# Output projection over pairs of token tiles by Strassen's scheme, with operands in slots of finished heads

## The chip, the cores and the metric

One core of one Trainium2 chip. The metric is device time of the whole program in microseconds (us), the median of repeated runs. The engines are named as in the profile: PE (matmuls; PEld is its weight loads), DVE, ACT and POOL (elementwise work), and SP, which here only issues DMAs. A queue's own entries carry a q (SPq).

## The reference

Two independent parts, written side by side into a 2048 x 1152 output, all fp32:

```python
# A: 32 heads of 18 features, in 4 segments of 512 tokens
q, k, v = x @ wq, x @ wk, x @ wv
for s in range(4):
    p = softmax(qs @ ks.T * scale + mask)          # mask of one segment
    o = g * (phi(qs) @ M / (phi(qs) @ z)) + (1 - g) * (p @ vs)
    M, z = M + phi(ks).T @ vs, z + phi(ks).sum(0)
a = concat(o) @ wo                                 # 2048 x 576 by 576 x 576
# B: real part of a two-dimensional Fourier transform by matrices
y = Cr @ (x @ Dr.T) - Ci @ (x @ Di.T)              # Cr, Ci: 2048 x 2048
out = concat([a, y], axis=-1)
```

The line that the change concerns is `concat(o) @ wo`.

## The kernel before

All precise products are split: an fp32 operand is cut into a high part that PE takes as it is and a low part (the rest), and a product is the sum of low x high, high x low and high x high. The 576 features are four chunks of 128 and a last one of 64; that last one is stored twice over 128 partitions (`_tail_twice`), so that high and low half share one operand and two matmuls do.

A first phase (to about 240 us) projects q, k, v and looks up the memory. A second phase runs two streams in one program order. `dense()` is part B as a generator: for `ri` 0 and 1, 16 steps of `hidden`, then 16 of `sequence`, whose left operand comes in chunks (`c_load`, `c_cut`: a load to `craw`, four buffers, then `chi` by ACT and `clo` by POOL). `attention()` goes over `NP` = 64 pairs of heads, one period of eight yields each, with stages that lag: `s_fill` in the pair's own period, `f_fill` and `t_fill` 2 and 3 periods later, the products with V (`pv`) 4 later. A loop advances `attention`, and then `dense` as long as its share of estimated time is behind. `later(n, ...)` puts a call n ticks on. What `dense` has left after the last period runs alone. Every engine takes its instructions in program order; all DMAs but a few are issued by SP in program order, the transposing DMAs of `f_turn` (L789) among them.

`wo` is loaded and split in the second half of `sequence` for `ri` = 1 (`wo_load`, L715, `wo_split`, which uses `split_wk`, L124 to L130), into ten slots of the pool `wide` (32 slots of 128 x 576) that the Fourier weights have left. The attention result lies in DRAM (`od`, `odt`), transposed. The output stage is the last loop: for each of 16 token tiles of 128, `o_split` makes `oth`, `otl`, `ott` of a tile loaded two tiles ahead (`o_load`, L695 and L697: one DMA for 512 features, two for the last 64), and for each half of the 576 output columns `chain` (L84) sums 14 matmuls of 128 x 128 by 128 x 288 in one bank `d`. ACT copies the bank to `y` (L1025), and four DMAs store a tile's rows (L1031):

```python
for k in range(4):
    terms += [(hi[:, k], wl[k][:, cs]), (hi[:, k], wh[k][:, cs]), (lo[:, k], wh[k][:, cs])]
chain(o, terms + [(tl, wt1[:, cs]), (tl, wt2[:, cs])])
act.activation(y[:, cs], o, AF.Copy)
```

`open_output` gives back the attention's pool `sa` before that and opens a new one, `sb3`, for the stage. The query and key stacks of head groups (`qs0` to `qs3`, `ks0` to `ks3`) are single buffers in `sr` and `sa`.

Of the kernel before, what the change touches and what calls it, by code (L numbers as in the profile page):

```python
# [12 lines left out]
F32 = mybir.dt.float32  # L13
F32R = mybir.dt.float32r
# [3 lines left out]
OP = mybir.AluOpType  # L18
# [22 lines left out]
def infini_attention_and_fnet(ctx: ExitStack, tc: tile.TileContext, xT, wqk, w8, wv, wo, beta, xtT, cT, hT, out):  # L41
# [16 lines left out]
    def split(hi, lo, raw, lo_engine=None):  # L58
        act.activation(hi, raw, AF.Copy)
        (lo_engine or dve).tensor_tensor(lo, raw, hi.bitcast(F32), OP.subtract)  # L60
# [80 lines left out]
    def weight(mk):  # L141
        return [[mk() for _ in range(4)] for _ in range(2)] + [mk() for _ in range(2)]
# [543 lines left out]
    O, O3, OT, WO, WORAW = {}, [], {}, [], []  # L686

    def o_load(t):  # L690
        if t >= NT:
            return
        s, a = divmod(t, 4)
        o = O3[0].tile([P, 5, P], F32, name="o", bufs=3) if O3 else sb.tile([P, 5, P], F32, name="raw", tag="raw", bufs=3)
        dma(o[:, :4], od[s][:, a * P:a * P + P].rearrange("c p x -> p c x"))  # L695
        for i in range(2):
            dma(o[64 * i:64 * i + 64, 4], odt[s][64 * a:64 * a + 64])  # L697
        O[t] = o

    def o_split(t):  # L700
        if t >= NT:
            return
        o_load(t + 2)
        o = O.pop(t)
        hi = O3[0].tile([P, 4, P], F32R, name="oth", bufs=2)
        lo = O3[0].tile([P, 4, P], F32R, name="otl", bufs=2)
        tl = O3[0].tile([P, P], F32R, name="ott", bufs=2)
        split(hi, lo, o[:, :4])
        act.activation(tl, o[:, 4], AF.Copy)
        dve.tensor_tensor(tl[64:], o[64:, 4], tl[64:].bitcast(F32), OP.subtract)  # L710
        OT[t] = hi, lo, tl

    def wo_load(k):
        raw = sb.tile([P, D], F32, name="raw", tag="raw", bufs=3)
        dma(raw, wo[k])  # L715
        WORAW.append(raw)

    def wo_split(k):
        if k == 0:
            WO.extend(weight(wide_tile(D)))  # L720
        split_wk(WO, k, WORAW.pop(0), 2)

    def open_output():
        p2a.close()
        O3.append(ctx.enter_context(tc.tile_pool(name="sb3", bufs=1, reuse_waits="tile")))

    p2a = ExitStack()
    sa = p2a.enter_context(tc.tile_pool(name="sb2a", bufs=1, reuse_waits="tile"))
    PT, PV = {}, {}


# [189 lines left out]
    def attention():  # L921
        for p in range(NP + V_LAG):
# [6 lines left out]
                    fn(2 * (p - lag) + 1, *a)  # L929

            if p < 2:
                stacks(sa, p + 2)
# [58 lines left out]
    while due:  # L991
        tick()
    td = ta = 0.0
    for w in attention():
# [18 lines left out]
    for t in range(NT):  # L1013
        o_split(t + 1)
        hi, lo, tl = OT.pop(t)
        y = O3[0].tile([P, D], F32, name="y3", bufs=2)
        for h in range(2):
            cs = slice(h * 288, h * 288 + 288)
            o = ps.tile([P, 288], F32, name="d", bufs=3)
            terms = []  # L1020
            wh, wl, wt1, wt2 = WO
            for k in range(4):
                terms += [(hi[:, k], wl[k][:, cs]), (hi[:, k], wh[k][:, cs]), (lo[:, k], wh[k][:, cs])]
            chain(o, terms + [(tl, wt1[:, cs]), (tl, wt2[:, cs])])
            act.activation(y[:, cs], o, AF.Copy)  # L1025
            if h or t == NT - 1:
                cs = cs if t == NT - 1 else slice(0, D)
                for q in range(4):
                    r = 512 * (t // 4) + P * q + 32 * (t % 4)
                    queue = nc.scalar if h and t == NT - 1 and q >= 2 else nc.sync  # L1030
                    queue.dma_start(out[r:r + 32, cs], y[32 * q:32 * q + 32, cs])  # L1031


_INS = ("xT", "wqk", "w8", "wv", "wo", "beta", "xtT", "cT", "hT")
# [38 lines left out]
```

## Time and profile before

| | |
|---|---|
| median of 3 runs | 998.46 us (997.72 to 999.36) |
| span of the profiled execution | 996.2 us; no time of its own outside the span is given for it |
| median less span | 2.3 us |
| granted PE clock | 0.999 of full speed |
| PE, DVE, ACT, POOL busy | 99%, 76%, 71%, 64% of the span |
| PE's instructions | 9294 matmuls, each with a weight load |
| DMA | 208.92 MB, 80.8% of 16 engines' time |

Busy time is the union of an engine's instructions. A matmul's own duration (some 290 ns here) overlaps with its neighbours', so the price of a matmul is the distance between starts, not its duration. Rows of the chain give a start, a duration, the engine, the tile and the line. Rows of groups give count, busy time and mean duration in ns, and behind the bar the idle time before them with what ended it.

### The profile page before, as it was taken

The numbers are of one execution on the slowest core, as the hardware profiler recorded it, in microseconds if no ns is written. First come the engines' busy times: TensorE is split into PE (matmuls) and PEld (weight loads), VectorE is DVE, ScalarE is ACT, GpSimd is POOL, SyncE is SP. The second block draws the span as 40 slices with busy tenths as digits, with TensorE's granted clock in tenths as the row PEclk, the third lists the DMA queues.
The fourth block names the chain that finished last, engine by engine and source line by source line (L and its number), as shares of the span: only waits on it lengthen the run. The fifth ranks groups of instructions, "written<-read, shape, count | busy, mean of one in ns | idle before, by whom it ended". The sixth has DMA issues, their size and how long they took to land.

```text
span 996.2 us, 25590 instructions
## 1 busy us (share of the span) xinstructions
PE 986.1 (99%) x9294; PEld 924.1 (93%) x9294; DVE 753.5 (76%) x2052; ACT 712.0 (71%) x1680; POOL 636.3 (64%) x700
## 2 busy tenths in 40 slices
PE   9999999999999999999999999999999999999998
PEld 8989989899999999999999999999999999999998
DVE  6657667594678777888898888888889899998321
ACT  7757575653887877878788888877777787777243
POOL 2657676675767677666766777766766767667000
PEclk9999999999999999999999999999999999999999
DMA  7537456767588898899999988779999999989455
GB/s 252 187 117 257 172 180 242 234 232 228 150 174 217 215 251 222 207 237 215 245 238 238 222 214 199 178 200 226 230 216 229 238 235 242 240 191 200 128 148 142
DMA packets 305615, 208.92 MB, mean 210 GB/s; under 512 B 206289, under 2 KB 260433, under 8 KB 305489
## 3 DMA queue, kind: packets, MB, share of 16 engines
q1 hardware_dynamic: 305248, 207.15, 80.8%
q8 instruction: 73, 1.20, 0.5%
q14 instruction: 54, 0.43, 0.2%
q10 hardware_dynamic: 240, 0.14, 0.0%
HBM read 121.32 MB, written 57.93 MB: 180 GB/s over the span
## 4 chain that ended last, share of the span: by engine, by line
PE 84%; DVE 6%; ACT 5%; issue 2%; DMA 2%; POOL 1%; SPq 0%; POOLq 0%; DVEq 0%; ACTq 0%
PE d L583 38%; PE s L744 7%; PE d L84 6%; PE v L84 4%; PE pv L862 4%; PE qk L250 4%; PE d L628 3%; PE d L629 3%; PE d L630 3%; PE pv L863 2%; PE m L363 1%; PE t L818 1%; PE qk L84 1%; DVE r L276 1%; PE t L821 1%
## 5 line engine op out<-in xcount | busy, mean ns | idle before, releaser
L750 DVE CUSTOM_DVE_ANT_0 s<-s,causal 128x128 f32<-128x128 f32 (+3 forms) x512 | 248.1, 504 | 94.0 <-PE s L744 84.8
L456 POOL TENSOR_TENSOR clo<-craw,chi 128x512 fp32r<-128x512 f32 x158 | 217.1, 1374 | 94.4 <-ACT chi L451 66.4
L583 PE MATMUL d<-wide,chi 128*128 128x288 f32 x1408 | 261.7, 303 | 0.0
L583 PEld LDWEIGHTS d<-wide,chi 128*128 128x128 f32 x1408 | 210.7, 188 | 2.7 <-issue 1.1
L583 PE MATMUL d<-wide,clo 128*128 128x288 f32 x704 | 173.3, 313 | 0.0
L784 POOL TENSOR_TENSOR hl<-pf,hl 128x768 f16<-128x768 f32 x64 | 112.6, 1759 | 69.3 <-ACT hl L780 58.7
L830 ACT ACTIVATE phi<-t 128x384 f16<-128x384 f32 x128 | 61.8, 483 | 103.8 <-PE t L827 103.8
L744 PE MATMUL s<-ks,qs 108*128 108x128 bf16 (+3 forms) x512 | 132.8, 303 | 2.7 <-DVE negm L750 2.1
L773 ACT ACTIVATE pf<-s,nb 128x128 f32<-128x128 f32 (+3 forms) x256 | 128.3, 527 | 6.2
L583 PE MATMUL d<-ab,chi 128*128 128x288 f32 x640 | 123.3, 302 | 0.0
L845 DVE TENSOR_TENSOR plo<-pf,phi 128x384 f16<-128x384 f32 (+1 forms) x128 | 122.9, 960 | 0.0
L583 PEld LDWEIGHTS d<-wide,clo 128*128 128x128 f32 x704 | 117.8, 189 | 1.9 <-issue 0.5
L451 ACT ACTIVATE chi<-craw 128x512 fp32r<-128x512 f32 x160 | 100.2, 627 | 6.1 <-DMA craw<-xtT 3.3
L831 ACT ACTIVATE pf<-t 128x384 f32<-128x384 f32 (+1 forms) x192 | 99.5, 518 | 5.9 <-PE t L818 5.5
L583 PEld LDWEIGHTS d<-ab,chi 128*128 128x128 f32 x640 | 97.8, 189 | 0.5
L780 ACT ACTIVATE hl<-pf 128x768 f16<-128x768 f32 (+1 forms) x128 | 87.4, 729 | 2.0
L583 PE MATMUL d<-ab,clo 128*128 128x288 f32 x320 | 83.0, 308 | 0.0
L628 PE MATMUL d<-wide,chi 128*128 128x288 f32 x256 | 81.3, 318 | 0.0
L629 PE MATMUL d<-wide,chi 128*128 128x288 f32 x256 | 75.7, 296 | 0.0
L630 PE MATMUL d<-wide,clo 128*128 128x288 f32 x256 | 75.6, 295 | 0.0
L845 POOL TENSOR_TENSOR plo<-pf,phi 128x384 f16<-128x384 f32 x64 | 61.4, 959 | 13.8 <-ACT pf L831 13.3
L784 DVE TENSOR_TENSOR hl<-pf,hl 128x512 f16<-128x512 f32 x64 | 69.4, 1084 | 0.1
(214 smaller groups left out, 2500.1 us busy)
## 6 DMA issues: line engine op xcount, KB each, us to landing
craw<-cT SPq DMA_DIRECT2D x128, 256.0 KB
ks<-kd SPq DMA_DIRECT2D x32, 432.0 KB
qs<-qd SPq DMA_DIRECT2D x32, 432.0 KB
craw<-xtT SPq DMA_DIRECT2D x32, 320.0 KB
vd<-vs SPq DMA_DIRECT2D x16, 440.0 KB
vst<-vd SPq DMA_DIRECT2D x32, 220.0 KB
qd<-p SPq DMA_DIRECT2D x16, 384.0 KB
kd<-p SPq DMA_DIRECT2D x16, 384.0 KB
```

What stands on the lines that cost most here:

```text
L84: pe.matmul(o, a, b, start=n == 0, stop=n == len(terms) - 1)
L451: act.activation(hi, raw[:, :4], AF.Copy)
L456: engine.tensor_tensor(lo, raw[:, :4], hi.bitcast(F32), OP.subtract)
L583: pe.matmul(o[h], a, b[:, h * 288:h * 288 + 288], start=start, stop=stop)
L628: pe.matmul(o, xh[:, k], wl[k][:, cs], start=k == 0, stop=False)
L629: pe.matmul(o, xh[:, k], wh[k][:, cs], start=False, stop=False)
L630: pe.matmul(o, xl[:, k], wh[k][:, cs], start=False, stop=False)
L744: pe.matmul(o[:, c:c + w], q[:, i * P:w], k[:, :w], start=True, stop=True)
L750: dve.tensor_tensor_reduce(o[:, c:c + w], o[:, c:c + w], CAUSAL[0][:, L - w:], scale=scale, scalar=-LOWEST, op0=OP.add, op1=OP.min, accum_ ...
L773: act.activation(f[:, FIRST_COL[i]:FIRST_COL[i] + w], o[:, c:c + w], AF.Exp, bias=nb[:, i:i + 1], scale=-1.0)
L784: engine.tensor_tensor(hl[:, 1, a:b], f[:, a:b], hl[:, 0, a:b], OP.subtract)
L845: (pool if kind == 2 else dve).tensor_tensor(lo[:, a:b], f[:, a:b], hi[:, a:b], OP.subtract)
```

## The change

The first 512 features of two token tiles, n and n + 8, form a left matrix of two by two blocks (tile by half of the features), and `wo` one of two by two blocks (half of the features by half of the columns). Strassen's scheme in Winograd's form computes the product with seven block products instead of eight: sums S1 to S4 of left blocks, T1 to T4 of right blocks, products P1 to P7, and sums of these. A block of the left has two chunks of 128 features, so a product is 2 x 3 matmuls of 128 x 288. The last 64 features are added the ordinary way with two matmuls for each of the four results, put on the product that goes into that result alone (`tail`); one needs a difference of two weight parts (`TAIL[0]`).

- `right_operands` replaces `wo_load` and `wo_split`: a generator, advanced once a yield in the last eight periods of `attention` (`n >= 8 * (NP - 4)`, which counts from period 60), that loads `wo`, splits B11, B21, B22 (`plain`), the tails and T1 to T4 (`combined`), in `wide` and in slots of `qs`, `ks` whose heads are finished. It ends with loads for pair 0 and its left operand.
- `left(n)` makes a pair's left operands from raw tiles: sums by POOL (DVE for pair 0), high parts by ACT, low parts by DVE, in eight `wide` slots.
- `output_stage` goes over eight pairs. P4 and P3 of a pair come one pair later. Banks: `s` for P1 + P2, `t` for P6, P7, P4, `d` for P5 and P3. Evacuation adds on DVE (five a pair) or copies on ACT (two).
- Loads of pair n + 2 go to `craw`; the order of store DMAs follows the products. `open_output` and `sb3` are gone; stacks 2 and 3 lie in a new pool `sq`.

```diff
-                if ri and 0 <= late < 5:
-                    wo_load(late)
-                if ri and 1 <= late < 6:
-                    wo_split(late - 1)
...
+        def plain(c):
...
+            for hi, lo, a in ((b11[:, 0], b11[:, 1], raw[c][:, :288]), (b2[0], b2[1], raw[c + 2])):
+                act.activation(hi, a, AF.Copy)
+                yield
+                pool.tensor_tensor(lo, a, hi.bitcast(F32), OP.subtract)
+                yield
...
+        def combined(c):
...
+            pool.tensor_tensor(b11, b12, b11, OP.subtract)
+            yield
+            dve.tensor_tensor(b12, b22, b12, OP.subtract)
+            yield
+            pool.tensor_tensor(b22, b22, b11, OP.subtract)
+            yield
+            dve.tensor_tensor(b21, b21, b22, OP.subtract)
+            yield
+            for names, r, hi, lo in ((("T1", "T3"), a, *to[:2]), (("T4", "T2"), b, *to[2:])):
+                act.activation(hi[0], r, AF.Copy)
+                yield
...
+                    dve.tensor_tensor(l, r[:, at:at + w], hi[0][:, at:at + w].bitcast(F32), OP.subtract)
...
+        for k in (0, 2, 4):
+            load(k)
+            yield
+        yield from pause(5)
+        yield from plain(0)
+        yield from tails()
+        load(1)
+        yield from pause(15)
+        yield from combined(0)
+        load(3)
+        yield from pause(3)
+        yield from plain(1)
+        yield from combined(1)
...
+        yield from pause(4)
+        yield from left(0)
+
+    def left(n):
...
+        add.tensor_tensor(t[:, 0], two[:, :2], two[:, 2:4], OP.add)
+        act.activation(ah, one[:, :4], AF.Copy)
+        yield
+        dve.tensor_tensor(t[:, 2], one[:, :2], two[:, :2], OP.subtract)
+        dve.tensor_tensor(al, one[:, :4], ah.bitcast(F32), OP.subtract)
+        act.activation(a22[:, :2], two[:, 2:4], AF.Copy)
+        yield
+        add.tensor_tensor(t[:, 1], t[:, 0], one[:, :2], OP.subtract)
+        dve.tensor_tensor(a22[:, 2:], two[:, 2:4], a22[:, :2].bitcast(F32), OP.subtract)
+        act.activation(tl[:, 0], one[:, 4], AF.Copy)
+        act.activation(tl[:, 1], two[:, 4], AF.Copy)
+        yield
+        add.tensor_tensor(t[:, 3], one[:, 2:4], t[:, 1], OP.subtract)
+        act.activation(s1, halves[0], AF.Copy)
+        yield
+        dve.tensor_tensor(l1, halves[0], s1.bitcast(F32), OP.subtract)
+        act.activation(s2, halves[1], AF.Copy)
+        for i, o in enumerate((one, two)):
+            add.tensor_tensor(tl[64:, i], o[64:, 4], tl[64:, i].bitcast(F32), OP.subtract)
+        yield
+        dve.tensor_tensor(l2, halves[1], s2.bitcast(F32), OP.subtract)
+        yield
+
+    def seventh(o, n, x, w, first=False, tail=None):
+        hi, lo = LEFT[n][x]
+        terms = []
+        for c in range(2):
+            wh, wl = WO[w, c]
+            terms += [(hi[:, c], wl), (hi[:, c], wh), (lo[:, c], wh)]
+        if tail:
+            terms += [(LEFT[n][tail[0]], m) for m in TAIL[tail[1]]]
+        for i, (a, b) in enumerate(terms):
+            pe.matmul(o, a, b, start=first and i == 0, stop=True, skip_group_check=True)
...
+        def p7(n):
+            u = U[n]
+            seventh(u[5], n, "S3", "T3", tail=(2, 2))
+            yield
+            dve.tensor_tensor(u[1][:, C], u[5], u[0][:, C], OP.add)
+            dve.tensor_tensor(u[3][:, Z], u[6], u[1][:, C], OP.add)
...
+        for n in range(8):
+            todo = [(p1, n), (p6, n), (p4, n - 1), (p5, n), (p3, n - 1), (p7, n), (p2, n)]
+            if n == 7:
+                todo += [(p4, n), (p3, n)]
+            if n < 6:
+                o_pair(n + 2)
+            prepare = left(n + 1) if n < 7 else iter(())
+            for fn, k in todo:
+                if k < 0:
+                    continue
+                piece = fn(k)
+                next(piece)
+                next(prepare, None)
+                next(piece, None)
+            for _ in prepare:
+                pass
...
-            if p == NP + 1:
-                o_load(0)
-                o_load(1)
...
+        if n >= 8 * (NP - 4):
+            next(ready, None)
...
-    open_output()
     for t in d:
         tick()
-        td += t or 0.0
-        if 0 in O and td > total_d - 3000.0:
-            o_split(0)
+        next(ready, None)
+        if not c_raw and 1 not in O:
+            o_pair(1)
```

More of the change, by code (lines that the diff above doesn't have):

```diff
@@ L679, in dense, with o_load @@
                     h_split(1, late - 1)
-                if ri and 0 <= late < 5:
-                    wo_load(late)
-                if ri and 1 <= late < 6:
-                    wo_split(late - 1)
                 yield from sequence(ri, tt)
[L686 to L692, printed above, removed]
+    O, LEFT, WO, TAIL = {}, {}, {}, {}
+    def o_load(t, tile_of):
         s, a = divmod(t, 4)
-        o = O3[0].tile([P, 5, P], F32, name="o", bufs=3) if O3 else sb.tile([P, 5, P], F32, name="raw", tag="raw", bufs=3)
+        o = tile_of()
         dma(o[:, :4], od[s][:, a * P:a * P + P].rearrange("c p x -> p c x"))
@@ L698, in o_load @@
         O[t] = o
[L700 to L716, printed above, removed]
@@ new lines, in seventh, with store @@
+    def seventh(o, n, x, w, first=False, tail=None):
[8 more added lines that the diff above has]
+            pe.matmul(o, a, b, start=first and i == 0, stop=True, skip_group_check=True)
+    def store(t, y, cs, last=False):
+        for q in range(4):
+            r = 512 * (t // 4) + P * q + 32 * (t % 4)
+            queue = nc.scalar if last and q >= 2 else nc.sync
+            queue.dma_start(out[r:r + 32, cs], y[32 * q:32 * q + 32, cs])
@@ L729, in infini_attention_and_fnet @@
+    sq = ctx.enter_context(tc.tile_pool(name="sb2q", bufs=1, side="right", reuse_waits="tile"))
+    sa = ctx.enter_context(tc.tile_pool(name="sb2a", bufs=1, reuse_waits="tile"))
     PT, PV = {}, {}
@@ L931, in attention @@
             if p < 2:
-                stacks(sa, p + 2)
+                stacks(sq, p + 2)
                 OG.append(sa.tile([P, 4, 72], F32, name=f"og{p}"))
@@ L993, in infini_attention_and_fnet @@
     td = ta = 0.0
-    for w in attention():
+    ready = right_operands()
+    for n, w in enumerate(attention()):
         tick()
         ta += w
+        if n >= 8 * (NP - 4):
+            next(ready, None)
         while td / total_d < ta / total_a:
@@ L1003, in infini_attention_and_fnet @@
         tick()
-    open_output()
     for t in d:
         tick()
-        td += t or 0.0
-        if 0 in O and td > total_d - 3000.0:
-            o_split(0)
+        next(ready, None)
+        if not c_raw and 1 not in O:
+            o_pair(1)
     while due:
         tick()
[L1013 to L1031, printed above, removed]
+    for _ in ready:
+        pass
+    output_stage()
 _INS = ("xT", "wqk", "w8", "wv", "wo", "beta", "xtT", "cT", "hT")
```

115 lines of the change are left out of this document (106 added, 9 removed).

## The prediction

> **What bounds the kernel now.** I read the page first, for the one engine that is full.
>
> ```profile
> span 996.2 us, 25590 instructions
> ...
> PE 986.1 (99%) x9294; PEld 924.1 (93%) x9294; DVE 753.5 (76%) x2052; ACT 712.0 (71%) x1680; POOL 636.3 (64%) x700
> ```
>
> PE works in 986.1 of 996.2 us. A stage therefore lasts as long as its matmuls, unless something else ends last in that stage. Then the chain of work that ended last, for the stage that is rewritten:
>
> ```profile
> 906.05 0.04 PE pv L862
> ...
> 928.01 4.33 PE d L583 x32
> 932.34 59.42 PE d L84 x448
> 991.78 0.41 ACT y L1025
> ```
>
> The output projection is one unbroken run of 448 matmuls from 932.34 to 991.76. Per matmul that is 59.42 / 448 = 132.6 ns. Call 932.34 T0. The span ends at 996.2, T0 + 63.9. So 4.4 us follow the last matmul, though the last evacuation takes only 0.41. The timeline of SP's DMA issues shows why:
>
> ```profile
> 933.41 0.42 SPq L695 DMA_DIRECT2D o<-od  x1
> 933.88 1.22 SPq L697 DMA_DIRECT2D o<-odt  x2
> ...
> 951.59 2.90 SPq L1031 DMA_DIRECT2D out<-y  x4
> ...
> 967.92 3.36 SPq L1031 DMA_DIRECT2D out<-y  x4
> ...
> 976.86 1.94 SPq L1031 DMA_DIRECT2D out<-y  x4
> 978.89 0.38 SPq L695 DMA_DIRECT2D o<-od  x1
> 979.32 1.20 SPq L697 DMA_DIRECT2D o<-odt  x2
> 980.62 1.94 SPq L1031 DMA_DIRECT2D out<-y  x4
> ...
> 984.38 9.74 SPq L1031 DMA_DIRECT2D out<-y  x18
> ```
>
> Four stores and three loads of a token tile take SP 980.62 - 976.86 = 3.76 us. PE's 28 matmuls of a tile take 28 x 0.1326 = 3.71. SP's queue is as full as PE. Three times it loses more: a group of stores takes 2.90 or 3.36 instead of 1.94 (0.96 and 1.42 lost), and the last 18 stores take 9.74 where 18 x 1.94 / 4 = 8.73 (1.0 lost), 3.4 us in all. From 951.59 to 984.38, eight tiles, it needed 4.10 us a tile and fell behind. It issues its last store until 994.12, 2.4 us after the last matmul, and the span ends 2.1 us behind that. So at the end of the stage SP's issue already closes the span, not PE.
>
> **Part by part.**
>
> *Fewer matmuls.* Before: 16 tiles x 2 halves x 14 = 448. After: each pair of tiles has seven products of 2 chunks x 3 terms = 42, and four tails of 2, so 50; eight pairs, 400. All keep the form 128x128 by 128x288, so 48 x 0.1326 = 6.4 us leave PE. PE's part would be 53.0 us, a pair 6.63. This is the gain if PE alone decides.
>
> *The same DMAs in less time.* Stores stay 68, of which 66 on SP. Twelve tiles are loaded inside the stage instead of thirteen. The first two pairs are loaded earlier, where SP has room behind the last transposing DMA. From T0 + 1.1, where the loads of pair 2 start, SP has 12 loads of 1.58 plus 0.1 (20.2), 15 full groups of 1.94 (29.1), six half-width stores (2.9 at the same price), 17 gaps of 0.1 (1.7): 53.9, and 57.3 with the three long ones again. That ends at T0 + 55.0 without them and T0 + 58.4 with them. I cannot see what makes an issue long; none came in the first 19 us of the old stage, so I take two of the three: T0 + 57.4. Before it was 994.12 - 932.34 = 61.8. The stage gains 4.4 us by SP, not 6.4: stores of the last pair come in three bunches (P2, P4, P3 of pair 7) close together, behind a backlog of some 4 us. The bounds are 3.4 (all three) and 7.1: none, and PE's own end, 53.0 plus an evacuation (0.46, the row of L653 below) and two issues, 54.7 with the hand-overs.
>
> The Trainium skill (DMA: Bandwidth & Descriptors, Issuing engines are not separate DMA queues) says that issue time is usually small beside the transfer. By it SP would not matter, and the end would be PE's, a gain of 6.4. The trace here disagrees: the issues are back to back at 3.76 us a tile.
>
> *Does the backlog reach PE?* Loads of pair n+2 stand in SP's queue ahead of the stores of pair n-1, so they slip with it. The last, pair 7, are issued by T0 + 40.0 (1.1, 20.2 of loads, 16.3 of stores, two long ones of 1.2), their main part 1.2 before. With 2.1 us to land, as at the end of the span, it is there at T0 + 40.9. The iteration that uses it starts after 34 + 5 x 50 matmuls, at T0 + 37.7. ACT and DVE wait in order there, and evacuations queue behind: P6's comes after two operations of the new operand (0.42 and 0.69, below) and takes 0.46, so it ends at 42.5. PE wants that bank for P7, 34 matmuls into the iteration, at 42.2. So a stall of 0.3, bounds nothing and 1 us; all of it lies under SP's own end (57.4 against 53.0). I take zero.
>
> *New work beside the matmuls.* Rows of the output stage by form, when POOL had no work there:
>
> ```profile
> L1025 ACT ACTIVATE y<-d 128x288 f32<-128x288 f32 x32 | 12.8, 411 | 35.3 <-PE d L84 26.9 <-DMA out<-y 5.3 <-ACT ott L709 3.1
> ...
> L60 DVE TENSOR_TENSOR otl<-o,oth 128x512 fp32r<-128x512 f32 x14 | 9.7, 692 | 38.6 <-ACT oth L59 38.6
> L59 ACT ACTIVATE oth<-o 128x512 fp32r<-128x512 f32 x14 | 8.8, 628 | 3.2 <-DMA o<-od 3.2
> L709 ACT ACTIVATE ott<-o 128x128 fp32r<-128x128 f32 x14 | 4.2, 300 | 1.2 <-DVE otl L60 1.2
> L710 DVE TENSOR_TENSOR ott<-o,ott 64x128 fp32r<-64x128 f32 x14 | 4.1, 289 | 1.2 <-ACT ott L709 0.8
> L653 DVE TENSOR_TENSOR y<-y,d 128x288 f32<-128x288 f32 x2 | 0.9, 455 | 0.6 <-PE d L583 0.6
> ```
>
> A 256-wide DVE operation lies between 289 and 692: 0.42 in proportion. DVE per pair: three of 512 (2.08), two of 256 (0.85), five evacuations like L653 (2.28): 5.2 of PE's 6.63 us. ACT: three of 512 (1.88), one of 256 (0.41), two tails (0.60), two evacuations (0.82): 3.7. The wait is that evacuations stand behind operand work on DVE, but they have 2.7 to 2.9 us each before PE writes the bank again. POOL's prices, from the page and the groups by form:
>
> ```profile
> L456 POOL TENSOR_TENSOR clo<-craw,chi 128x512 fp32r<-128x512 f32 x158 | 217.1, 1374 | 94.4 <-ACT chi L451 66.4
> ...
> L458 POOL TENSOR_TENSOR xtail<-craw,xtail 64x128 fp32r<-64x128 f32 x30 | 14.8, 492 | 2.4
> ```
>
> Three of 256 (0.79 by proportion) and two tails of 0.49 are 3.3 us a pair. They do not only lie beside DVE's. The timeline of POOL, then of DVE:
>
> ```profile
> 913.13 1.67 POOL L784 TENSOR_TENSOR hl<-pf,hl 128x768 f16<-128x768 f32 x1 [1.92 <-ACT hl L780]
> ```
> ```profile
> 913.36 1.99 DVE L845 TENSOR_TENSOR plo<-pf,phi 128x512 f16<-128x512 f32 x1
> ```
>
> The 512-wide subtraction on DVE took 1.99 us where L60 takes 0.692: it starts 0.23 us into POOL's operation and ends 0.55 behind it, so it waits until POOL is through. Five such DVE operations a pair can meet five POOL ones. Nothing waited: 5.2. All of POOL waited out: 5.2 + 3.3 = 8.5. POOL's first three run back to back when their tiles land, so I count two meetings of 0.6: 6.4, just under 6.63. The Trainium skill (GPSIMD Engine Reference, Key points) says POOL shares its SBUF interfaces with VectorE, to the cost of instructions with two SBUF inputs; the pair of rows agrees, and the rule speaks against this change.
>
> *Work moved in the attention phase.* The preparation of the right operand leaves the earlier part and goes to the last eight periods:
>
> ```profile
> L124 DVE TENSOR_TENSOR wide<-raw,wide 128x576 fp32r<-128x576 f32 x8 | 11.8, 1471 | 0.0
> ```
> ```profile
> 888.80 0.75 DVE L126 TENSOR_TENSOR wide<-raw,wide 64x576 fp32r<-64x576 f32 x1
> 889.58 0.76 DVE L127 TENSOR_TENSOR wide<-raw,wide 64x576 fp32r<-64x576 f32 x1
> ...
> 904.24 1.38 DVE L845 TENSOR_TENSOR plo<-pf,phi 128x512 f16<-128x512 f32 x1
> ```
>
> Removed from DVE: four of 1.47 and these two, 7.4 us. Added in the last periods with queries to score: the tails (two of 0.75, two of about 0.4), 2.3. Added behind them: twice four or five DVE operations (2.5 a chunk of the weights), some 9 us on POOL over all, 4 more 576-wide ones on ACT, and the first left operand (4.4 on DVE) in the last period. That last lies beside the dense rest (4.33 us, 32 matmuls); its parts for P1 and P6 are done before T0, so no gap. What lies on the path is DVE's subtraction at 904.24: it ends at 905.62 and the first product with V that reads it is at 906.05, slack 0.4 us. Ahead of it come 2.5 us of new DVE work and about 1 of waiting for POOL; 1.5 (888.80 to 890.34) and idle of some 0.6 are freed: about 1.4, less the 0.4, so 1.0 us of PE stall. How often PE waited for DVE before:
>
> ```profile
> PE s L744 <- DVE negm L750: 1.2, 4, 0.4
> ```
>
> (from 300 us to 932). Taking the 1.47s out of the earlier, fuller periods can give back about half of that, 0.6. So T0 moves by +0.4, bounds -0.7 and +2.5 (all new DVE work on the path). The two loads of weights that now wait for a free slot hold SP's queue, with the transposing DMAs behind; those have whole periods of slack, so nothing.
>
> *Sum.* Profiled span 996.2 + 0.4 - 4.4 = 992.2. The median of the runs, 998.46, is 2.3 above the span, which stays: **994.5 us**.
>
> **The rivals.**
> 1. *PE alone decides.* SP's long issues do not come back. Stage -6.4 to -7.1, T0 from -0.7 to +0.4: 990.7 to 992.5, typically 991.6. For it: they are three of some hundred. Against: they came at even distances, so they belong to issuing.
> 2. *The attention phase gives the gain back.* T0 +2.5, and stores held up by late loads for 1 to 2 us more: 996.5 to 998.5, say 997.5. For it: DVE has 0.4 us of slack at 905.62 and POOL gets 9 us. Against: the reductions for the row maxima (`s_fill`) have ended by then, by the loop's bounds.
> 3. *DVE becomes the bound: slower.* Each POOL operation meets a two-input one on DVE. At 8.5 us a pair, eight pairs are 68 against 59.4; with 2 us less tail, since SP then keeps pace, 998.46 + 8.6 - 2 = 1005. It costs time from 59.4 / 8 = 7.4 us a pair on, which is 2.2 of the 3.3 us waited out. Against: only part of POOL's work can meet, and evacuations read PSUM.
> 4. *Not doing what it says:* 400 matmuls instead of 448 follow from the loops; I give this no chance of its own.
>
> **How the numbers follow.** About 0.2%, 2 us, is what a measurement here can tell from no change. Forecast 0.50 (992.5 to 996.5); rival 1 0.20; rival 2 0.20; rival 3 0.10. Faster holds the forecast, rival 1 and a little of rival 2: 0.72. Same: the rest of rival 2, 0.18. Slower: 0.10. The range leaves out rival 3 and the far end of rival 1: 990.8 to 999.8.
>
> **What would show it.** Right: 400 matmuls from the new helper on `s`, `t` and `d`, at 133 ns, with no stall over 1 us; PE's stage of 53 to 54 us starting within 1 us of 932.7; SP's issues unbroken to about 57 us after T0, 3 to 4 us behind the last matmul; DVE's 512-wide subtractions between 0.7 and 1.5 us; PV waits on DVE's subtraction in the periods behind 890. Wrong: a stage of over 57 us on PE, with PE waiting for DVE (rival 3) or for ACT behind a load (SP reaching PE); a T0 later than 935; or SP done within 2 us of PE (rival 1).

## The result and the profile after

The changed kernel is slower. Its median is 1010.5 us (1009.8 to 1012.7, 4 runs), against 998.1 for the kernel before, measured beside it (4 runs): ratio 1.0129, 95% interval 1.0113 to 1.0144. The forecast was 994.5 with a range to 999.8. The profiled execution spans 1009.0 us, 12.8 more than before.

The top of the page shows that the matmuls did go, and that PE is no longer full:

```profile
span 1009.0 us, 25590 instructions
...
PE 984.3 (98%) x9246; PEld 921.7 (91%) x9246; DVE 786.2 (78%) x2112; ACT 714.8 (71%) x1686; POOL 675.6 (67%) x744
```

9294 - 9246 = 48 matmuls fewer. PE now stands still for 24.7 us of the span; before it was 10.1. The 12.8 us lie in three places.

| us | before | after | difference |
|---|---|---|---|
| T0, the first output matmul | 932.34 | 938.32 | +6.0 |
| first to last output matmul | 59.42 | 61.04 | +1.6 |
| last output matmul to the end of the span | 4.4 | 9.6 | +5.2 |

**The last periods of attention (+6.0).** The waits of PE from 840 us to T0, each with total, count and longest:

```profile
PE pv L1052 <- DVE plo L1034: 1.7, 2, 1.4
PE d L583 <- DVE y L653: 1.7, 1, 1.7
PE pv L1051 <- DVE og L1073: 1.3, 1, 1.3
PE s L933 <- ACT pf L962: 1.2, 1, 1.2
```

They sum to 5.9 us (the kernel before stood still for 0.9 us from 840 to 920 and not at all from there to T0), and three of the four are waits for DVE. The fourth goes back to POOL: ACT stood for 2.1 us before POOL's difference of the tails (L733), with the probabilities that PE waited for behind it. What DVE does ahead of the last waits, on its timeline:

```profile
923.65 3.00 DVE L764 TENSOR_TENSOR late<-raw,wide 128x288 fp32r<-128x288 f32 x2
926.58 0.20 DVE L1064 RECIPROCAL pv<-pv 128x8 f32<-128x8 f32 x1
...
928.23 0.68 DVE L1034 TENSOR_TENSOR plo<-pf,phi 128x512 f16<-128x512 f32 x1
```

Two subtractions of `combined(1)` (L764) take 3.00 us, and the normalisation and the low part of the probabilities, for which PE waits, stand behind them. On POOL's timeline two `clo` run from 923.27 to 926.34, over the same stretch.

**The stage (+1.6 instead of -6.4).** PE's timeline at T0, with the idle time before a group and what ended it in brackets:

```profile
938.32 0.96 PE L841 MATMUL s<-wide,l 128*128 128x288 f32 x6
...
939.90 0.96 PE L841 MATMUL d<-late,l 128*128 128x288 f32 x6
945.41 1.81 PE L841 MATMUL t<-late,l 128*128 128x288 f32 x6 [4.55 <-DVE u L864]
947.01 0.68 PE L841 MATMUL t<-wide,lb 128*128 128x288 f32 x2
```

After three products PE waits 4.55 us for DVE's evacuation of P6. DVE and SP then:

```profile
943.43 0.42 DVE L812 TENSOR_TENSOR ls<-craw 128x256 f32<-128x256 f32 x1 [4.33 <-DMA craw<-od]
943.77 1.22 DVE L813 TENSOR_TENSOR wide<-craw,wide 128x512 fp32r<-128x512 f32 x1
944.91 0.45 DVE L864 TENSOR_TENSOR u<-t,u 128x288 f32<-128x288 f32 x1
```
```profile
937.64 0.34 SPq L94 DMA_DIRECT2D od<-ogt  x1
938.07 0.39 SPq L94 DMA_DIRECT2D odt<-oglt  x1
938.55 0.40 SPq L687 DMA_DIRECT2D craw<-od  x1
939.00 1.14 SPq L689 DMA_DIRECT2D craw<-odt  x2
940.25 0.53 SPq L687 DMA_DIRECT2D craw<-od  x1
```
```profile
SPq L94 <- DVE oglt L1098: 10.0, 1, 10.0
...
SPq L847 <- DMA out<-u: 4.9, 1, 4.9
```

The evacuation (L864) stands on DVE behind two operations of pair 1's left operand, and these wait for pair 1's loads. The loads stand on SP behind the last two stores of attention, where SP waits 10.0 us for DVE's last transposes. So pair 1 is loaded from 938.55 on, after T0.

When PE resumes, it is slow. Six matmuls from 945.41 to 947.01 are 267 ns each, twice 132.6. The windows (columns: length, then busy time and instructions of PE, PEld, DVE, ACT, POOL, then granted clock, DMA share, GB/s):

```profile
920.00:930.00 10.00, 7.38 (x84) 7.00 (x85) 9.62 (x18) 3.81 (x8) 6.34 (x6) 0.99 0.73 175
930.00:940.00 10.00, 10.00 (x81) 9.93 (x81) 6.24 (x18) 1.26 (x2) 0.61 (x1) 0.83 0.07 22
940.00:950.00 10.00, 5.45 (x26) 5.22 (x25) 4.66 (x8) 3.43 (x9) 5.52 (x8) 0.68 0.67 190
950.00:990.00 40.00, 39.41 (x296) 39.19 (x295) 31.24 (x58) 18.73 (x48) 21.71 (x27) 1.00 0.57 150
```

The granted clock is 0.83 and 0.68 behind the gaps, and 1.00 again from 950 on, where PE takes 133 ns a matmul as before (296 in 39.41 us). In narrower windows it is 0.50 from 929.9 to 933.3 and from 943.5 to 950.4. An estimate from that: the first stretch, 3.4 us at half rate, costs 1.7 us of the 6.0, and the 5.0 us of the second in which PE works cost 2.5 us of the stage. With the gap of 4.55 us and a later one of 0.6 at 988.2 that makes 7.6 of the 8.0 us that lie between the +1.6 measured and the -6.4 of the matmuls alone.

**The tail (+5.2).** SP's wait of 4.9 us (L847, above) is the third store of P3 of pair 6. It ends at 1001.42, behind the two stores on ACT's queue:

```profile
999.89 0.82 ACTq L847 DMA_DIRECT2D out<-u  x2
```

The trace keeps for every DMA the completion semaphore that it raises and those that it waits for: from 985 us on the DMAs of both queues take eight semaphores in turn, and a DMA waits for the one before it on its semaphore. SP's store at 1001.42 waits for the semaphore of ACT's store at 999.89. So ACT's two stores of P3 of pair 7 come ahead of SP's last two stores of P3 of pair 6 in that order, though they are issued behind the last evacuation, and SP waits there for a store of a later block, with 11 more behind it.

### The profile page after: what moved, and what is told of

Read it like the earlier page. It is cut to its first block, busy times and chain, and to the rows that moved or that the text cites. A ratio compares the mean times of both kernels' runs of the same rounds, so it can differ in the third digit from the quotient of the medians.

```text
span 1009.0 us, 25590 instructions
## 1 busy us (share of the span) xinstructions
PE 984.3 (98%) x9246; PEld 921.7 (91%) x9246; DVE 786.2 (78%) x2112; ACT 714.8 (71%) x1686; POOL 675.6 (67%) x744
## 4 chain that ended last, share of the span: by engine, by line
PE 77%; DVE 7%; ACT 4%; POOL 3%; issue 3%; DMA 3%; SPq 1%; POOLq 0%; DVEq 0%; ACTq 0%
PE d L583 35%; PE s L933 7%; PE v L84 4%; PE pv L1051 4%; PE qk L250 4%; PE d L630 3%; PE d L628 3%; PE d L629 3%; PE pv L1052 2%; DMA craw<-od 2%; PE m L363 1%; PE qk L84 1%; PE t L1007 1%; PE t L841 1%; DVE r L276 1%
## 5 line engine op out<-in xcount | busy, mean ns | idle before, releaser
L456 POOL TENSOR_TENSOR clo<-craw,chi 128x512 fp32r<-128x512 f32 x158 | 219.7, 1391 | 88.6 <-ACT chi L451 61.8
L1034 DVE TENSOR_TENSOR plo<-pf,phi 128x384 f16<-128x384 f32 (+1 forms) x128 | 118.6, 927 | 0.0
```

The source lines that it names most:

```text
L456: engine.tensor_tensor(lo, raw[:, :4], hi.bitcast(F32), OP.subtract)
L1034: (pool if kind == 2 else dve).tensor_tensor(lo[:, a:b], f[:, a:b], hi[:, a:b], OP.subtract)
```

## The experiments

All are measured beside the kernel before, on the same chip. "Tail" is the time from the last output matmul to the end of the span. The program parts that all kernels share already lie up to 2.6 us apart at 700 us between profiled executions, so differences of T0 under 2 us say little. Span, T0, stage and tail are of one execution, and others of the same kernel lie up to 4.4 us from it in span; what an edit is worth is better read from the ratios, where 0.001 is 1.0 us.

| run | ratio to before, 95% interval | span | T0 | stage | tail |
|---|---|---|---|---|---|
| changed kernel | 1.0129 (1.0113 to 1.0144) | 1009.0 | 938.3 | 61.0 | 9.6 |
| e1_stores_sp | 1.0097 (1.0082 to 1.0112) | 1004.8 | 937.5 | 61.4 | 5.9 |
| e2_pair1_early | 1.0064 (1.0047 to 1.0080) | 1004.0 | 938.9 | 56.4 | 8.7 |
| e3_no_right_arith | 1.0082 (1.0067 to 1.0097) | 1005.0 | 931.1 | 63.8 | 10.1 |
| e3b_no_low1 | 1.0112 (1.0091 to 1.0133) | 1005.9 | 935.0 | 61.3 | 9.6 |
| e4_stores_and_loads | 1.0042 (1.0026 to 1.0057) | 1001.5 | 939.0 | 56.6 | 5.9 |
| e5_early | 1.0095 (1.0081 to 1.0109) | 1004.8 | 940.1 | 58.9 | 5.9 |
| e6_loads_act | 1.0083 (1.0071 to 1.0096) | 1004.1 | 941.1 | 57.1 | 6.0 |
| e7_no_arith_e4 | 1.0013 (1.0004 to 1.0022) | 994.9 | 930.6 | 57.9 | 6.4 |
| e8_right_on_dve | 1.0105 (1.0087 to 1.0123) | 1004.2 | 941.0 | 56.8 | 6.4 |
| e9_no_pool | 1.0060 (1.0045 to 1.0076) | 1001.7 | 939.1 | 56.2 | 6.4 |
| e10_no_dve | 0.9993 (0.9983 to 1.0002) | 996.3 | 932.1 | 58.4 | 5.9 |
| e11_dve_spread | 1.0074 (1.0062 to 1.0087) | 1003.8 | 938.1 | 59.3 | 6.4 |
| e12_right_on_pool | 1.0096 (1.0080 to 1.0111) | 1004.7 | 940.5 | 58.2 | 5.9 |
| e13_pool_spread | 1.0069 (1.0056 to 1.0081) | 1002.8 | 940.6 | 56.2 | 6.1 |
| e14_pool_loads_act | 1.0060 (1.0047 to 1.0074) | 1003.9 | 942.9 | 55.1 | 5.9 |
| e15_pool_slots | 0.9986 (0.9975 to 0.9998) | 994.3 | 933.2 | 55.1 | 6.1 |
| e17_tail_pool | 0.9979 (0.9962 to 0.9997) | 993.7 | 933.9 | 54.4 | 5.4 |
| e18_left0_pool | 0.9969 (0.9958 to 0.9980) | 993.2 | 932.6 | 55.3 | 5.4 |

**e1_stores_sp: the tail.**

```diff
-            queue = nc.scalar if last and q >= 2 else nc.sync
-            queue.dma_start(out[r:r + 32, cs], y[32 * q:32 * q + 32, cs])
+            nc.sync.dma_start(out[r:r + 32, cs], y[32 * q:32 * q + 32, cs])
```

> All stores of the last tile go through SP's queue; ACT's queue takes none. Theory (the tail): in the changed kernel SP's third store of the last-but-one row block waited 4.9 us for a store on ACT's queue that stands later in time but earlier in the order of completion lanes. Without stores on ACT's queue that wait goes to under 0.5 us. SP then issues 12 to 16 stores back to back at 0.45 to 0.55 us from 996.5 on, so the last is issued at about 1003 to 1004 instead of 1006.9: the span goes from 1009.0 to 1005 or 1006, 3 to 4 us less. Rival (the 4.9 us is a wait for the transfer itself, the write to memory being slow there): the wait stays, and with two more stores on SP the span is 1 us longer. Start of the output stage (938.3) and the stall of 4.55 us in pair 0 stay as they are under both.

SP's last 26 stores are one run now, 0.49 us each:

```profile
989.93 12.73 SPq L846 DMA_DIRECT2D out<-u  x26
```

Tail 9.6 to 5.9, span -4.2 (3.2 us by the ratios): the wait was for ACT's later store, not for the transfer of SP's own.

**e2_pair1_early: the stall.**

```diff
+        o_pair(1)
         yield from pause(4)
         yield from left(0)
...
-        if not c_raw and 1 not in O:
-            o_pair(1)
```

> The six loads of pair 1 (token tiles 1 and 9) stand in SP's queue right behind those of pair 0, ahead of the last two stores of attention results, instead of behind them. Theory (the load): PE's stall of 4.55 us at P6 of pair 0 came from loads issued at 938.6 to 942 instead of about 928; the stall falls under 1 us, the granted clock behind it no longer drops to 0.68 (another 1 to 2.5 us), and the span goes from 1009.0 to 1002 to 1004. Rival (DVE's and ACT's own work on the left operand of pair 1 stands ahead of the evacuation, load or not): the stall stays over 2.5 us and the span gains under 2.5 us.

The timeline of SP, and PE's group that had waited 4.55 us:

```profile
928.47 0.53 SPq L687 DMA_DIRECT2D craw<-od  x1
```
```profile
941.58 1.06 PE L842 MATMUL t<-late,l 128*128 128x288 f32 x6 [0.16 <-DVE u L865]
```

The loads come 10 us sooner, the stall is 0.16 us with no fall of the clock behind it, the stage is 4.7 us shorter (6.5 us of the time by the ratios). DVE's own operand work was not what held the evacuation here.

**e3_no_right_arith and e3b_no_low1: the late T0.** The first leaves out every `tensor_tensor` of `right_operands` (low parts point to the high ones), the second only this one, for the second chunk:

```diff
-                    dve.tensor_tensor(l, r[:, at:at + w], hi[0][:, at:at + w].bitcast(F32), OP.subtract)
+                    if c == 0:
+                        dve.tensor_tensor(l, r[:, at:at + w], hi[0][:, at:at + w].bitcast(F32), OP.subtract)
```

> Left out of the computation: all additions and subtractions that make the right operands (the sums of weight blocks and the low parts), in the last eight periods of attention; the high part stands in for the low one, so matmuls, loads, ACT's copies and the left operands are as before. Theory (DVE and POOL work on the weights delays attention): the output stage begins at 931 to 933 instead of 938.3, and with no gap ahead of it the clock of the stretch 930 to 940 is back over 0.95; span 1001.5 to 1003. Rival (the delay is the first left operand's work on DVE and the loads of weights that hold SP's queue): the stage begins at 936 or later, span 1006 or more. Stall in pair 0 and the tail stay as they are.

> Left out of the computation: only the low parts of the four combined right operands of the second chunk (three subtractions on DVE, of 576, 288 and 288 columns, around 920 to 927 us); the high part stands in. Theory: those two of 288 columns took 1.5 us each, waiting for POOL, ahead of the last normalisations and probabilities; they carry the last 3.4 us of the attention phase's delay, so the output stage begins at 934.5 to 936 instead of 938.3, span 1005 to 1006.5. Rival (the delay was already there and only shows at the end, because attention waits for something else): under 1 us.

T0 falls by 7.2 us in the first and by 3.3 in the second: the arithmetic for the right operands is all of the delay, and the three late subtractions nearly half. The span gains only 4.0 in the first, because pair 1's loads still wait for attention's last stores: the stall in pair 0 grows to 6.6 us. I had expected it to stay, and a span of 1001.5 to 1003 with it. By its ratio the second run is not clearly faster than the changed kernel: the intervals overlap.

**e4_stores_and_loads** (both edits of e1 and e2).

> Both edits together: all stores on SP's queue, and pair 1's loads ahead of the last stores of attention. Theory (two separate causes): the gains add, 4.2 and 5.0 us of the span, so 999 to 1001 instead of 1009.0; stage begins at 938 to 939, 56 to 57 us long, last store issued about 3.5 us behind the last matmul. Rival (both uncover the same bound, SP issuing 14 transfers a pair back to back): less than 7 us together, span 1002 or more.

7.5 us off the span, where 4.2 + 5.0 would be 9.2, and 8.7 by the ratios, where 3.2 + 6.5 would be 9.7: nearly the sum, though the span is half a microsecond worse than the theory's bound. This is the base of the runs below. What stays is T0 = 939.0.

**e5_early and e6_loads_act: is it the place of the work?** Plain parts and first sums from period 52 on (`START` is 12); splits as soon as slots are free:

```diff
+        yield from first_half(0)
+        yield from second_half(0)
+        yield from tails()
+        load(1)
+        yield from sums(0)
+        yield from first_half(1)
+        yield from until(60, 6)
+        q0, k0 = late(0, "q"), late(0, "k")
+        yield from parts(0, 0, ("T1", "T3"), [q0[:, :D]], [k0[:, :D]])
...
-        if n >= 8 * (NP - 4):
+        now[0] = n
+        if n >= 8 * (NP - START):
```

e6 adds `nc.scalar` as queue for two of a pair's six loads.

> As the run before with the same two edits, and the right operands made earlier: loads and plain parts from period 52 of attention on instead of 60, sums of the first chunk right behind them, the splits of the combined operands as soon as the slots of the heads' groups 28 and 29 are free (periods 60.8 and 62.8), in such slots and one of the weights' own, so that none waits for group 30 and nothing of it falls behind period 63; pair 0 is loaded into slots of groups 29 and 30 at period 64.8. The arithmetic is the same. Theory (the same work costs nothing where attention is bound by PE, and costs its length in the last four periods, where the chain of waits runs through DVE): the stage begins at 931 to 933.5, no fall of the clock before it; span 992 to 995.5. Rival (the work costs the same wherever it stands, because DVE and POOL are short of time all along): stage begins at 936 or later, span over 997.

> As the run before, and of the six loads of each pair from 2 on, the two for the last 64 features of the second tile are issued on ACT's queue (some 1.2 us of issuing a pair moved from SP, where 14 issues of a pair take 6.6 to 6.9 us against PE's 6.63). Theory (SP's issue rate is what is left behind the stage): the stalls of about 1 us at pairs 6 and 7 go, the stage is 53.5 to 55 us, and the last store is issued 1 us sooner behind the last matmul: 1.5 to 3 us less than the run before. Rival (ACT's evacuations of P1 and P2 come later behind its issues): the stage is longer by 1 to 3 us.

A miss. T0 is 940.1 and 941.1, no earlier than in e4. PE is idle for 4.4 us between 860 and 900 in e5, against 1.2 in e4: the same work costs as much in earlier periods, so the place alone was not the cause. The stage is longer than e4's because the first left operand begins only at period 67.75: in pair 0 of e5 PE waits 1.1 us for it and 1.8 us for an evacuation that stands behind left operand work on DVE. e6's stage is 1.7 us shorter than e5's, its last store comes no sooner behind the last matmul (3.8 us in both), and the intervals of the two ratios overlap.

**e7_no_arith_e4** (e4 with e3's cut).

> The two edits of the stores and of pair 1's loads, with the additions and subtractions for the right operands left out of the computation (high parts stand in for the low ones), at the changed kernel's places otherwise. It shows what is left with all three causes gone. Theory: stage begins at 931 to 932, 55 to 57 us long, no stall of over 1.2 us in pair 0, tail as with the stores on SP; span 992 to 994.5. Rival (something else in the stage holds it, such as the left operands of pair 1, which must then be made in less time): a stall of over 2 us in pair 0 stays and the span is over 996.

T0 (930.6) and the profiled span (994.9) lie 0.4 us outside the theory's ranges, the stage (57.9) 0.9 us, and the other nine executions span 996.2 to 999.1 us. PE waits 2.5 us in pair 0. Both were the rival's signs: with T0 earlier, DVE's work on both first left operands does stand ahead of the evacuation. The ratio is 1.0013: with these two edits alone the kernel would not be faster even if this arithmetic cost nothing.

**e8_right_on_dve, e9_no_pool, e10_no_dve: which engine?** In e8 the POOL operations of `right_operands` go to DVE in place. e9 leaves out those on POOL, e10 those on DVE. My theory was POOL's queue.

```diff
-                pool.tensor_tensor(lo, a, hi.bitcast(F32), OP.subtract)
+                dve.tensor_tensor(lo, a, hi.bitcast(F32), OP.subtract)
```

> The kernel with the two edits of stores and loads (stage from 939.0, span 1001.5), and the right operands' operations that were on POOL (four low parts, one difference of the tails, four differences of weight blocks; some 9 us there) put on DVE at the same places in the program. Theory (POOL's queue is what delays attention: its operations stand ahead of the four short ones that turn the row maxima around, and DVE's subtractions wait while POOL runs): though DVE gets 5 to 6 us more, the stage begins at 933 to 936, span 995.5 to 998.5. Rival (DVE is the engine short of time): the stage begins at 940 to 943, span over 1002.

> As the kernel with the two edits, with the right operands' POOL operations left out of the computation, and DVE's kept. With all of them left out the stage began at 930.6 instead of 939.0: 8.4 us to be shared between POOL and DVE. Theory (POOL): 5 us or more of it go, stage from 931 to 934. Rival (DVE): under 3 us go, stage from 936 or later.

> The counterpart: the right operands' DVE operations left out of the computation, POOL's kept. Theory (POOL): the stage still begins at 935 to 939, at most 4 us earlier. Rival (DVE): at 931 to 934.

The first output matmul of e9, then of e10:

```profile
939.11 0.96 PE L838 MATMUL s<-wide,l 128*128 128x288 f32 x6
```
```profile
932.09 0.96 PE L837 MATMUL s<-wide,l 128*128 128x288 f32 x6
```

The theory fell. Without POOL's operations (10.9 us in the changed kernel) T0 does not move (939.1 against 939.0); without DVE's it is 932.1, 6.9 us sooner; with POOL's share put on DVE it is 2.0 later. By the ratios e10 is 4.9 us faster than e4, and e9 is not clear of it. The longest waits of PE from 840 to 945 us in e9 are all for DVE, now for the row maxima too (`negm`); the wait that goes back to POOL is gone:

```profile
PE pv L1048 <- DVE plo L1030: 2.4, 2, 1.4
PE s L929 <- DVE negm L935: 2.0, 1, 2.0
PE d L583 <- DVE y L653: 1.7, 1, 1.7
```

**e11_dve_spread, e12_right_on_pool, e13_pool_spread, e14_pool_loads_act: DVE's time, or any arithmetic?** e11 and e13 spread the work from period 43 on, one operation a period (two from 60.8 on), on DVE alone and on POOL alone; e12 and e14 put it on POOL in the changed kernel's places, e14 with e6's two loads on ACT's queue. From e13:

```diff
+        def beat():
+            yield
+            while now[0] < 10 ** 6 and now[0] % 8 not in ((5,) if now[0] < 480 else (2, 5)):
+                yield
...
+            yield from beat()
+            pool.tensor_tensor(b11, b12, b11, OP.subtract)
```

> The full computation again: right operands made as in the run with the early preparation, but by DVE and ACT alone, and spread: one DVE operation a period from period 43 on, two a period from 60.8 on, behind the first maxima of a period; for that three chunks of weights are loaded at period 41, and chunks 1 and 3 twice. Theory (POOL's queue, not the amount of work): stage begins at 931.5 to 934, span 992 to 996. Rival (any 15 us of work on DVE and POOL cost about half of it or more, wherever they stand): the stage begins at 937 or later, span over 999.

> The kernel with the two edits of stores and loads, and the right operands' thirteen DVE operations put on POOL at the same places in the program; POOL then has some 23 us of them. The result is the full computation. Theory (DVE's time alone carries the delay): the stage begins at 931 to 934 instead of 939.0, span 993.5 to 996.5. Rival (POOL fills up: it was at 16 to 17 of each 20 us there, and what it takes more of delays attention's own subtractions on it, and DVE's behind them): the stage begins at 936 or later, span over 998.

> The early and spread schedule of the run before last, with all the right operands' arithmetic on POOL instead of DVE: one operation a period from period 43, two from 60.8 on. Theory: as POOL has more room early (13 to 14.5 of 20 us), the stage begins at 931 to 933, and no later than with POOL at the late places; span 992.5 to 996. Rival (POOL's operations delay the row maxima wherever they stand): stage begins at 936 or later, as with DVE spread.

> The first of these three, and of the six loads of each pair from 2 on, the two for the last 64 features of the second tile issued on ACT's queue. Theory (SP issues 14 transfers a pair in 6.6 to 6.9 us against PE's 6.63, and loads behind stores come late): PE's two stalls at pairs 6 and 7 (0.7 and 1.6 us) go and the last store is issued about 1 us sooner behind the last matmul: 2 to 3 us less than the first. Rival (ACT, whose evacuation of P1 stands behind its issues, holds PE): no gain, or up to 2 us more.

By T0 all four are late, and the theory's numbers missed, but not for one reason. PE's waits for the row maxima from 600 us on, first e11, then e13:

```profile
PE s L971 <- DVE negm L977: 4.3, 8, 1.4
```
```profile
PE s L971 <- DVE negm L977: 1.5, 3, 0.9
```

Spread on DVE, the work makes PE wait eight times, 4.3 us in all; spread on POOL, three times, 1.5 us. In e13 PE is busy for 40.00 of the 40 us from 880 to 920. In e12, with all of it on POOL in the last eight periods, the rival is right, POOL fills up (busy for 9.84 of the ten us from 920 on). The first of these waits goes back to POOL as well: ACT stands 4.3 us before POOL's difference of the tails, 2.1 in the changed kernel.

```profile
PE s L933 <- ACT pf L962: 3.4, 1, 3.4
PE d L583 <- POOL clo L456: 3.2, 2, 2.2
```

e13 loses its gain behind 918, on ACT, then DVE:

```profile
926.15 0.42 ACT L853 ACTIVATE lb<-oraw 128x256 fp32r<-128x256 f32 x1 [7.42 <-DMA ptt<-hl]
```
```profile
926.66 0.43 DVE L856 TENSOR_TENSOR lb<-oraw,lb 128x256 fp32r<-128x256 f32 x1 [4.60 <-ACT lb L853]
```

I had started the first left operand 1.25 periods sooner than in e11, and one of its tiles lies in a slot that a transposing DMA still reads. ACT waits for that slot, DVE for ACT, and the last products with V for both. e14's stage is 3.1 us shorter than e12's: stalls of 1.2, 0.4, 0.8 and 1.5 us become 0.6 and 0.7 (the 1.2 and the 0.6 lie in pair 0, ahead of the moved loads). Two loads of six off SP's queue help, as expected there, 3.6 us by the ratios, but the tail stays at 5.9: the last store does not come sooner behind the last matmul.

**e15_pool_slots, e17_tail_pool, e18_left0_pool: put together.** e15 is e13 with that tile and the sums in slots of the last head group, and with e6's loads; e17 has two stores of P4 of pair 7 on POOL's queue; e18 also has the first left operand's sums on POOL. From e15, then e18:

```diff
-            b = sa.tile([P, 6, P], F32R, name="lb", tag="hl", bufs=2)
+            b = sq.tile([P, 4, 256], F32R, name="late", tag="qs3").rearrange("p a x -> p (a x)")[:, :6 * P].rearrange("p (k x) -> p k x", k=6)
...
-        add = pool if n else dve
+        add = pool
```

> The right operands' arithmetic on POOL and spread, as two runs before; the first left operand's fifth tile and its sums now lie in the slots of the heads' group 31, free from period 66.5 on, instead of slots that a transposing DMA still reads; and two of six loads of a pair go on ACT's queue. Theory (the wait for that slot was all that was left of the delay): no wait of ACT or DVE over 2 us between 917 and 930; the stage begins at 931 to 933.5, is 55 to 56 us long, and the span is 992 to 995, less than 996.2 of the kernel before. Rival (the four microseconds of DVE work for the first left operand in the last two periods delay the last products with V in any slot): the stage begins at 935 or later, span over 996.

> As the run before, and two of the four stores of the last tile but one row block (P4 of pair 7) on POOL's queue. Theory (behind the last matmul SP issues the eight stores of two blocks at 0.45 us each, and nothing else is left): the last store on SP is issued 0.9 us sooner, span 0.5 to 0.9 us less. Rival (POOL takes longer to issue its two stores than SP the six that it keeps): the span is 0 to 2 us longer.

> As the run before, and the sums, one difference and the two tails of pair 0's left operand on POOL instead of DVE, as for every other pair (five operations, about 3.5 us of DVE between 917 and 928). Theory (DVE's time carries what is left of the delay): PE's 1.2 us wait for the probabilities' low part goes and the stage begins 0.5 to 1.5 us sooner, at 932.4 to 933.4; span 992.2 to 993.2. Rival (DVE then waits for POOL in its own two-input subtractions, as in the rest of the kernel): no gain within 0.5 us, or up to 1 us later.

T0 is 932.6 to 933.9, as the theory had it for e15 (933.2, span 994.3). All three are faster than the kernel before; e18's ratio is 0.9969 (0.9958 to 0.9980), its median 994.2 us. The windows of e18:

```profile
880.00:920.00 40.00, 40.00 (x456) 38.25 (x455) 33.99 (x82) 33.18 (x78) 36.97 (x36) 1.00 0.96 211
920.00:930.00 10.00, 9.83 (x105) 9.59 (x105) 8.44 (x16) 2.20 (x4) 8.26 (x8) 1.00 0.75 148
930.00:940.00 10.00, 10.00 (x77) 9.94 (x76) 5.83 (x15) 4.28 (x11) 3.44 (x6) 1.00 0.53 155
```

POOL carries 36.97 of 40 us there and PE does not wait; in the changed kernel PE was busy for 7.38 of the ten from 920 on. The clock stays at 1.00. e17's and e18's own steps are under 1 us each in span (0.6 and 0.5), in the direction expected, and each one's interval overlaps with that of the run before it: taken one by one their gains are not shown. What e18 does show is that PE's wait for the probabilities' low part goes from 1.2 to 0.2 us.

## Why the prediction was wrong, step by step

- *Fewer matmuls, 6.4 us:* right. 48 went, at 133 ns, and with the rest mended the stage takes 54.4 to 55.3 us instead of 59.4, near the 53.0 forecast for PE's part. e18 ends near the forecast (median 994.2 against 994.5), but it is another kernel: its right operands are made on POOL and in other periods, so this does not make the forecast right.
- *The attention phase, +0.4 (bounds -0.7 and +2.5):* the step that failed most; measured +6.0. I counted the slack before one DVE subtraction (0.4 us) and took DVE's other time as cover. e9 and e10 show that thirteen DVE operations cost 6.9 us, and in e5 and e11, where they stand elsewhere, T0 is hardly sooner. Their size was wrong as well: they took 15.2 us of DVE, where I had counted 2.3 and twice 2.5, or 7.3, about what was removed (7.4). A row that I had shown has 1.47 us for one subtraction of 576 columns, and yet I put the four or five operations of a chunk at 2.5 together. Those of 576 columns on all partitions took 0.9 to 1.5 us each, those of 288 took 0.9 to 1.9. Without POOL's right-operand work (e9) they still took 15.6, so that work was not what made them long. The work on POOL, which I had charged with about 1 us through DVE's waits, left T0 where it was. My upper bound "all new DVE work on the path" held only the work ahead of that one subtraction, not that of the later periods. "So no gap" ahead of T0 failed with it: PE was idle for 2.6 of the ten us behind 920, and the clock fell, which makes an estimated 1.7 of the 6.0.
- *"The first two pairs are loaded earlier, where SP has room behind the last transposing DMA":* wrong for pair 1. The last stores of attention stand ahead of it and hold SP for 10.0 us. I read SP's free time, not what its next instruction waits for. Cost, by e2: 5.0 us of the span, 6.5 by the ratios, the slow clock behind the stall with it.
- *SP's end at T0 + 57.4:* wrong, it issued stores until T0 + 68.6. The three closing bunches were foreseen, the wait for a store on the other queue not (e1: 4.2 us of the span, 3.2 by the ratios). With that gone and pair 1 loaded in time (e4) SP is done at T0 + 60.4. That SP's issue rate matters is borne out: two loads of six off its queue make e14's stage 3.1 us shorter than e12's and e6's 1.7 shorter than e5's. The rule of the Trainium skill that the prediction weighed (DMA: Bandwidth & Descriptors, Issuing engines are not separate DMA queues) does not hold for this stage.
- *Late loads reach PE by 0 to 1 us, taken as zero:* too low. In e4 the last two pairs stall PE for 0.7 and 1.6 us.
- *DVE 6.4 us a pair, rival 3:* refuted. From 950 to 990 us DVE is busy for 31.24 of 40 us, 5.2 a pair, what I had for no waiting at all.
- *Rival 2, attention gives the gain back:* the right mechanism at less than half its size, and its "against" (the row maxima are done by then) was beside the point: PE waited for the probabilities' low part, a normalisation and `y`. I gave it 0.20 and no way beyond 998.5. The wrong signs that I had named came: T0 later than 935 and a stage over 57 us.

## What to carry to other kernels

Before moving work into a stretch, ask which engine the bound engine already waits for there; its free share is no cover when its instructions are a chain, and another engine may do the same work without holding the bound one, if the work is spread (e18) and not bunched (e12). Price what is added by the same row as what is removed. For a load that is moved, follow the queue to the instruction just ahead and what that waits for. With stores on two queues, look at which completion a store waits for, not only at what it stores: the later block's store can hold the earlier one's.

## What the runs showed of the hardware

- PE's clock falls after short idle. Behind a gap of 4.55 us matmuls came 267 ns apart, twice 132.6; the clock was at half from 943.5 on, 2.7 us into the gap. The Trainium skill (TensorE: Matmul & The Clock Gate, Part 1) has half rate after an idle window of about 3.4 us, and this gap agrees. But the clock was also at half from 929.9 to 933.3, where PE had been busy for 1.8 of the 3.4 us before and no single gap there was over 1.3 us. In e15, with one wait of 1.2 us at 925.3, it stayed at 1.00. What decides inside such a stretch the runs do not show.
- Two-input subtractions on DVE do wait for POOL (3.00 us for two of 288 columns, beside POOL's 3.07, where another of 288 took 0.86). Even so, leaving out POOL's extra operations gained no time (e9), and leaving out DVE's did (e10).
